# Talking-heads attention and a gated feed-forward on one core: the loads of the values and of the conversion go from SyncE's queue to GpSimd's, the mix weights from GpSimd to ScalarE

## The chip, the core and the metric

The kernel runs on one core of a Trainium2 chip. A core has five engines, each with its own queue that is worked through in order: TensorE (PE in the profile, with its weight loads as PEld), VectorE (DVE), ScalarE (ACT), GpSimd (POOL) and SyncE (SP, which issues DMAs and computes nothing). The metric is the device time of one execution in microseconds (us). Of the kernel before there are three runs, median 1788.36 us, 1786.55 to 1803.96, and one profiled execution.

## The reference

Attention over 8 batches of 12 heads, 448 tokens and 64 columns a head. A 12 by 12 matrix mixes the heads of the scores, a softmax follows, a second 12 by 12 matrix mixes the heads of the softmax, and then come the values. The result goes through a feed-forward layer of width 2048 whose gate is h minus tanh(h).

```python
scores = scale * np.matmul(q, k.transpose(0, 1, 3, 2))
scores = np.einsum('bhij,hg->bgij', scores, w_pre)
scores = scores - np.max(scores, axis=-1, keepdims=True)
attn = np.exp(scores)
attn = attn / (np.sum(attn, axis=-1, keepdims=True) + 1e-09)
attn = np.einsum('bhij,hg->bgij', attn, w_post)
attn_out = np.matmul(attn, v).astype(np.float32)
x = np.ascontiguousarray(attn_out.transpose(0, 2, 1, 3)).reshape(B * S, H * D)
h = x @ moe_w_in
g = h - np.tanh(h)
return (g @ moe_w_out).astype(np.float32)
```

## The kernel before

**Two stages.** The first, about 855 us, is the attention; the second is the feed-forward. Beside the attention the kernel also converts the weights of the feed-forward, which arrive as 64-bit numbers, into pairs of 32-bit parts and stores them to DRAM.

**Places.** The attention takes its tokens in 32 blocks (8 batches of 120, 120, 120 and 88 tokens) and these in 360 groups of at most 10 tokens, whose 12 heads fill 120 partitions. Two groups make a place; there are 180 places, and the loop over `p` writes the work of one after the other. A place `p` holds, in this order: the copy `at` of the mix of two places back out of PSUM (L570, or two L577 where a block ends, ScalarE); the issue of queued DMAs; the first head mix `premix(p)` (L521, TensorE, into `ps_p`); `norm(p - 1)`; `expo(p)`, which is two row maxima `mx` (L530, VectorE) and two exponentials `e` (L532, ScalarE, which also sum into `zs`); the jobs planned for this place (scores of a later block L477, transposes of q L443 or k L417, values L602, all TensorE); and the second head mix `mix(p - 1)` (L560, TensorE, into `ps_o`), whose result ScalarE copies at the start of the next place.

**The mix weights.** The softmax isn't divided in its full size. `norm` adds 1e-9 to the sums (L541), takes their reciprocal (L542, both VectorE) and multiplies it into the 60 columns of the second mixing matrix `wpost`, once for each half of the place's rows: the tile `wr` (L543, one GpSimd instruction for both halves). `mix` uses `wr` as a matmul operand, so its first matmul waits for `wr`; and as `ps_o` has one buffer, it waits for the copy `at` of the mix before.

**The conversion.** `narrow_steps` works on 56 chunks, two at a time with a third loading. Each chunk has eleven steps, spread over VectorE, ScalarE (L82, L85, L102) and GpSimd (L96, L98, L104), and about four such steps are placed at the end of each place. A chunk's load is the tile `cr` (three buffers), its two results go to DRAM as `ws`. L102 on ScalarE reads what GpSimd's L98 made.

**Queues.** DMAs are put on two Python lists, `queue` (loads of q, k and v, stores of x) and `slow` (the conversion's loads and stores), and `issue(6)` sends at most six of them at each place. The gathers `t<-s` (L510) that bring the scores of a group's tokens together are issued just before, straight on SP. All of it goes through SP's queue, at L369. What stands in front of the loop (`now()`, the first k, q and v tiles) goes through SP too.

At the end every engine's instructions are pinned to the order in which the code writes them (`in_order`), so the order on each engine is that of the program text.

Of the kernel before, what the change touches and what calls it, by code (L numbers as in the profile page):

```python
# [18 lines left out]
DRAM = bass.MemoryType.DRAM  # L19
# [129 lines left out]
def kernel_body(  # L149
# [11 lines left out]
    nc = tc.nc  # L161
    B, H, S, D = q.shape
    P = 128
# [9 lines left out]
    HP = GH * H  # L173
# [165 lines left out]
    with ExitStack() as st:  # L339
# [17 lines left out]
        kks, vts, krs, qrs, qbs, sts, ats = {}, {}, {}, {}, {}, {}, {}  # L357


        queue, slow, sent = [], [], {}  # L360

        def dma(dst, src, to=None):
            entry = [place[0], dst, src, None]
            (queue if to is None else to).append(entry)
            return lambda places=0: entry[3] is not None and entry[3] + places <= place[0]

        def send(x, engine):
            entry = x.pop(0)
            engine.dma_start(*entry[1:3])  # L369
            entry[3] = place[0]  # L370

        def issue(most):
            for x in (queue, slow):
                while x and most and x[0][0] < place[0]:
                    send(x, nc.sync)
                    most -= 1

        place = [0]
# [7 lines left out]

        def load_v(b, hq):
            t = kp.tile([CP, 4, NC, D], F32, name="vr", tag="vr", bufs=3)
            sent[b, hq, "v"] = dma(
                t.rearrange("p h c d -> p h (c d)"),  # L390
                v[b, 4 * hq : 4 * hq + 4].rearrange("h (p c) d -> p h (c d)", c=NC),
            )
            vts[b, hq] = t

        def load_q(i, t=None):
# [140 lines left out]
        def norm(p):  # L536
            zs = te[p][1]
            wr = gp.tile([P, 2, D], F32, name="wr", tag="wr", bufs=2)[:, :, :HP]
            for r in range(2):

                nc.vector.tensor_scalar_add(zs[:, 1, r : r + 1], zs[:, 0, r : r + 1], 1e-9)  # L541
            nc.vector.reciprocal(zs[:, 2], zs[:, 1])  # L542
            nc.gpsimd.tensor_mul(  # L543
                wr, wpost[:, :HP].unsqueeze(1).to_broadcast([P, 2, HP]), zs[:, 2].unsqueeze(2).to_broadcast([P, 2, HP])
            )
            te[p].append(wr)

        def mix(p):
# [101 lines left out]
        for hq in range(3):  # L650
            load_v(0, hq)
# [32 lines left out]
        for w in range(2):  # L684
            for at in AT[w]:
                x = repeat[:, w, at : at + HP].rearrange("p (i h) -> p i h", i=GH)
# [5 lines left out]
        wpre, wpost = [cst.tile([P, D], F32, name=x) for x in ("wpre", "wpost")]  # L692
        both = tmp_w[:, 2 * P : 2 * P + 4 * HP].rearrange("p (w a n) -> p w a n", w=2, a=2)
        for w in range(2):
            for a in range(2):
                if w == 0:
                    x = both[:, w, a].rearrange("p (i g) -> p i g", i=GH)
                    of, step = ps_w[:, w, :].unsqueeze(1).to_broadcast([P, GH, H]), [[H, GH], [0, H]]
                else:
                    x = both[:, w, a].rearrange("p (g i) -> p g i", i=GH)  # L700
# [68 lines left out]
        while halved:  # L769
            ready = sorted((x for x in halved if x[0] <= p), key=lambda x: (x[1], x[3:]))  # L770
            if ready:
                x = ready[0]
# [3 lines left out]
                if x[2] == kind and other and x[1] > p + 1:  # L776
                    x = other[0]
# [9 lines left out]
        for i, (b, m) in enumerate(blocks):  # L787
            p0 = first[i] // 2
            if i + 2 < len(blocks):
                p = at_s[i + 2, 0] - 1  # L790
                at_place(p, prep_q, i + 2, 0)
                at_place(p, prep_q, i + 2, 1)
                if i + 3 < len(blocks):
                    at_place(p + 1, load_q, i + 3)
            if b and m == 0:
                for hq in range(NP // 2):
                    at_place(p0 + 4 + hq, load_v, b, hq)
# [34 lines left out]
        for p in range(NPL + 3):  # L832
# [4 lines left out]
            for t in (2 * p + 4, 2 * p + 5):  # L837
                if t < NG:
                    gather(t)
            issue(6)  # L840
            if p == NPL + 1:
                for f in start.pop(p):
# [3 lines left out]
            if 1 <= p < NPL + 1:  # L846
                norm(p - 1)
# [100 lines left out]
```

## Time and profile before

| what | value |
|---|---|
| median of 3 runs | 1788.36 us (1786.55 to 1803.96) |
| the profiled execution's own time | 1788.92 us |
| its span, first to last instruction | 1787.2 us |
| granted TensorE clock, mean | 0.993 |
| busy: PE, PEld | 1751.0 us, 1425.6 us |
| busy: DVE, ACT, POOL | 1128.3 us, 1000.5 us, 320.1 us |
| HBM read and written | 245.37 MB, 47.19 MB |

The page gives each engine's busy time, groups of equal instructions by source line, and who waited for whom. `A L1 <- B L2: total, times, longest` in a list of waits means that engine A stood idle before its line L1 until B's line L2 had finished. In a timeline a row gives the start, the duration, the engine, the line, the operation, and at its end in brackets the idle time before it. A line named Lxxx is one of the kernel before.

### The profile page before, as it was taken

The page shows a single profiled execution, that of the slowest core. Times are in us where ns is not written, and L with a number is a line of the kernel's source. Part 1 is how long each engine was busy: PE and PEld are TensorE (multiplying, and loading weights), DVE is VectorE, ACT ScalarE, POOL GpSimd, SP SyncE. Part 2 cuts the span into 40 slices and gives each one's busy share as a digit, 9 for nine tenths or more (in the row PEclk, how much of TensorE's full clock was granted, in tenths as well). Part 3 has the DMA queues.
Part 4 walks back from the last instruction along what each step waited for, and adds up shares of the span by engine and source line. Part 5 has one row for each costly group of instructions (what it writes and reads, how often), then busy time and mean ns, then how long its engine had stood idle before and what let it go on. Part 6 is the DMA issues. An engine that isn't in the chain of part 4 may idle for free.

```text
span 1787.2 us, 41382 instructions
## 1 busy us (share of the span) xinstructions
PE 1751.0 (98%) x16572; PEld 1425.6 (80%) x16572; DVE 1128.3 (63%) x2362; ACT 1000.5 (56%) x2051; POOL 320.1 (18%) x417
## 2 busy tenths in 40 slices
PE   8999999999999999999999999999999999999998
PEld 6777777777777777777888888888888888888887
DVE  5676777777777767664556566565565565655555
ACT  5777877777777776765343443433434434444333
POOL 1333333333333333321010010000000000000000
PEclk9999999999999999999999999999999999999999
DMA  8668687777967687565655655655656655655651
GB/s 176 204 196 216 194 236 224 217 215 215 249 203 218 215 213 220 178 202 216 255 207 194 248 193 207 241 193 214 229 197 216 224 208 204 228 217 190 230 194 36
DMA packets 232816, 372.32 MB, mean 208 GB/s; under 512 B 98992, under 2 KB 207536, under 8 KB 218288
## 3 DMA queue, kind: packets, MB, share of 16 engines
q1 hardware_dynamic: 231740, 368.45, 64.0%
q8 instruction: 131, 2.15, 0.5%
q10 hardware_dynamic: 884, 1.22, 0.2%
q14 instruction: 61, 0.50, 0.1%
HBM read 245.37 MB, written 47.19 MB: 164 GB/s over the span
## 4 chain that ended last, share of the span: by engine, by line
PE 87%; DMA 4%; ACT 4%; DVE 3%; issue 1%; POOL 0%; SPq 0%; ACTq 0%; DVEq 0%; POOLq 0%
PE ps_o L560 13%; PE ps_h L257 8%; PE ps_h L258 8%; PE ps_h L262 8%; PE ps_m L602 8%; PE ps_p L521 7%; PE ya L305 6%; PE ya L302 6%; PE ya L303 6%; PE ps_q L477 5%; PE yb L305 3%; PE yb L303 3%; PE yb L302 3%; DMA t<-s 2%; PE ps_m L443 1%
## 5 line engine op out<-in xcount | busy, mean ns | idle before, releaser
L560 PEld LDWEIGHTS ps_o<-wr,e 60*112 60x112 f32 (+1 forms) x5760 | 306.2, 176 | 44.3 <-POOL wr L543 21.8
L560 PE MATMUL ps_o<-wr,e 60*112 60x60 f32 (+1 forms) x5760 | 315.5, 259 | 14.3 <-POOL wr L543 7.7
L530 DVE TENSOR_REDUCE mx<-ps_p 128x1 f32<-128x448 f32 x360 | 207.7, 619 | 163.9 <-PE ps_p L521 163.7
L532 ACT ACTIVATE e<-ps_p,mx 128x448 f32<-128x448 f32 x360 | 225.7, 634 | 101.9 <-DVE mx L530 99.4
L289 ACT CAST gh<-r 128x512 fp32r<-128x512 f32 x112 | 69.6, 621 | 372.6 <-DVE r L282 372.6
L258 PE MATMUL ps_h<-xl,w 128*128 128x512 f32 x672 | 264.4, 393 | 0.0
L257 PE MATMUL ps_h<-xh,w 128*128 128x512 f32 x672 | 264.3, 393 | 0.0
L570 ACT COPY at<-ps_o 112x960 f32<-112x960 f32 x156 | 153.7, 985 | 93.8 <-PE ps_o L560 93.2
L247 POOL TENSOR_TENSOR xl<-rx,xh 128x512 fp32r<-128x512 f32 x38 | 55.6, 1464 | 731.2 <-ACT xh L246 731.2
L521 PE MATMUL ps_p<-t,wpre 60*64 60x448 f32 (+1 forms) x1440 | 180.8, 569 | 3.9 <-DMA t<-s 2.7
L305 PE MATMUL ya<-w,gl 128*128 128x512 f32 x448 | 177.0, 395 | 0.7 <-DVE gl L290 0.7
L278 DVE SCALAR_TENSOR_TENSOR r<-qa,ps_h 128x512 f32<-128x512 f32 x112 | 77.1, 688 | 159.2 <-ACT t L275 159.2
L302 PE MATMUL ya<-w,gh 128*128 128x512 f32 x448 | 174.8, 390 | 1.0 <-ACT gh L289 1.0
L303 PE MATMUL ya<-w,gh 128*128 128x512 f32 x448 | 174.8, 390 | 0.0
L602 PEld LDWEIGHTS ps_m<-at,vr 112*64 112x64 f32 x3072 | 147.5, 137 | 31.0 <-ACT at L577 10.9
L262 PE MATMUL ps_h<-xh,w 128*128 128x512 f32 x672 | 170.6, 389 | 0.0
L602 PE MATMUL ps_m<-at,vr 112*64 112x120 f32 (+1 forms) x3072 | 161.6, 261 | 8.4 <-ACT at L577 3.1
L272 ACT ACTIVATE u<-ps_h 128x512 f32<-128x512 f32 x112 | 67.0, 599 | 152.9 <-PE ps_h L262 152.9
L262 PEld LDWEIGHTS ps_h<-xh,w 128*128 128x128 f32 x672 | 126.3, 188 | 26.3
L258 PEld LDWEIGHTS ps_h<-xl,w 128*128 128x128 f32 x672 | 127.5, 190 | 23.7
L257 PEld LDWEIGHTS ps_h<-xh,w 128*128 128x128 f32 x672 | 127.4, 190 | 23.4
L543 POOL TENSOR_TENSOR wr<-wpost,zs 128x120 f32<-128x120 f32 x180 | 70.2, 390 | 402.9 <-DVE zs L542 293.6
(93 smaller groups left out, 3038.0 us busy)
## 6 DMA issues: line engine op xcount, KB each, us to landing
w<-ws SPq DMA_DIRECT2D x112, 1536.0 KB
t<-s SPq DMA_DIRECT2D x342, 210.0 KB
cr<-in_moe_w_in_dram SPq DMA_DIRECT2D x24, 512.0 KB
cr<-in_moe_w_out_dram SPq DMA_DIRECT2D x32, 384.0 KB
vr<-in_v_dram SPq DMA_DIRECT2D x24, 448.0 KB
kr<-in_k_dram SPq DMA_DIRECT2D x23, 448.0 KB
out_dram<-ob SPq DMA_DIRECT2D x24, 384.0 KB
qr<-in_q_dram SPq DMA_DIRECT2D x23, 360.0 KB
```

Of the source, the lines that this page charges most:

```text
L257: nc.tensor.matmul(ph, wh[:, fs], xh, start=(c == 0), stop=False)
L258: nc.tensor.matmul(ph, wh[:, fs], xl, start=False, stop=False)
L262: nc.tensor.matmul(ph, wl[:, fs], xh, start=False, stop=(c == NK - 1))
L302: nc.tensor.matmul(y, gh[:, tok], wh[:, es], start=first, stop=False)
L303: nc.tensor.matmul(y, gh[:, tok], wl[:, es], start=False, stop=False)
L305: nc.tensor.matmul(y, gl[:, tok], wh[:, es], start=False, stop=last)
L521: nc.tensor.matmul(pss[r][halves[j], :], wpre[k, :], ts[j][k, :], start=True, stop=True)
L530: nc.vector.tensor_reduce(out=mx, in_=ps, axis=AX.X, op=ALU.max, negate=True)
L532: nc.scalar.activation(e, ps, AF.Exp, bias=mx, scale=1.0, accum_out=zs[:, 0, r : r + 1])
L560: nc.tensor.matmul(ps[:CP, j, c * GP : (c + 1) * GP].rearrange("p (h i) -> p h i", i=GI)[:, :, r * GH : (r + 1) * GH], e[k, c * CP : (c + ...
L570: nc.scalar.copy(ats[i0][:, :, :, at : at + 2 * GI].rearrange("p c h (j i) -> p j (c h) i", j=2), ps[:CP, :, : NC * GP].rearrange("p j (x ...
L602: nc.tensor.matmul(pv[j * D : (j + 1) * D, r, :n], vt[:, j, c, :], ats[i][:, c, 2 * hp + j, :n], start=(c == 0), stop=(c == NC - 1),)
```

## The change

Two things are moved. The loads of the values (`vr`, from the second batch on) and of the conversion's chunks (`cr`) are issued from GpSimd's queue instead of SP's; the stores of the conversion and every other DMA stay on SP. And `wr` is made by ScalarE, with two instructions of 60 columns that each take the reciprocal as a per-partition scale, instead of one GpSimd instruction.

```diff
-        queue, slow, sent = [], [], {}
+        queue, slow, sent, of_v = [], [], {}, []
...
         def issue(most):
             for x in (queue, slow):
                 while x and most and x[0][0] < place[0]:
-                    send(x, nc.sync)
+
+                    apart = x[0][1].space != DRAM and (x is slow or any(x[0] is y for y in of_v))
+                    send(x, nc.gpsimd if apart else nc.sync)
                     most -= 1
...
         def load_v(b, hq):
             t = kp.tile([CP, 4, NC, D], F32, name="vr", tag="vr", bufs=3)
+            before = len(queue)
             sent[b, hq, "v"] = dma(
...
+            of_v.extend(queue[before:])
             vts[b, hq] = t
...
             nc.vector.reciprocal(zs[:, 2], zs[:, 1])
-            nc.gpsimd.tensor_mul(
-                wr, wpost[:, :HP].unsqueeze(1).to_broadcast([P, 2, HP]), zs[:, 2].unsqueeze(2).to_broadcast([P, 2, HP])
-            )
+            for r in range(2):
+                nc.scalar.mul(wr[:, r, :], wpost[:, :HP], zs[:, 2, r : r + 1])
             te[p].append(wr)
```

ScalarE's queue around places 40 and 41 (213 to 219 us of the profile), before. Each row is a line, an operation, what it writes and reads, and its shape; `at` is the copy of a mix, `e` the exponentials, `cm`, `cr` and `cs` are steps of the conversion:

```order
L82 ACTIVATE cm<-cm 128x384
L570 COPY at<-ps_o 112x2x48x10
L532 ACTIVATE e,zs<-ps_p,mx 128x448 x2
L85 ACTIVATE cr<-cr 128x384
L102 CAST cs<-cm 128x384
L577 COPY at<-ps_o 112x48x10 x2
L532 ACTIVATE e,zs<-ps_p,mx 128x448 x2
```

The same stretch of ScalarE's queue in the changed kernel (its lines are numbered 3 or 4 higher):

```order
L82 ACTIVATE cm<-cm 128x384
L573 COPY at<-ps_o 112x2x48x10
L548 ACTIVATE wr<-wpost,zs 128x60 x2
L536 ACTIVATE e,zs<-ps_p,mx 128x448 x2
L85 ACTIVATE cr<-cr 128x384
L102 CAST cs<-cm 128x384
L580 COPY at<-ps_o 112x48x10 x2
L548 ACTIVATE wr<-wpost,zs 128x60 x2
L536 ACTIVATE e,zs<-ps_p,mx 128x448 x2
```

The two instructions of `wr` stand between the copy of the previous mix and the exponentials, at each of the 180 places.

GpSimd's queue where the values of a later batch are loaded (about 348 to 377 us of the profile), before:

```order
L104 TENSOR_TENSOR cl<-cm,cs 128x384
L543 TENSOR_TENSOR wr<-wpost,zs 128x2x60
L96 TENSOR_TENSOR cm<-cr,cs 128x384
L98 TENSOR_TENSOR cm<-cm,cr 128x384
L543 TENSOR_TENSOR wr<-wpost,zs 128x2x60
L104 TENSOR_TENSOR cl<-cm,cs 128x384
L543 TENSOR_TENSOR wr<-wpost,zs 128x2x60 x2
L96 TENSOR_TENSOR cm<-cr,cs 128x384
L543 TENSOR_TENSOR wr<-wpost,zs 128x2x60
L98 TENSOR_TENSOR cm<-cm,cr 128x384
```

The same stretch of GpSimd's queue in the changed kernel, where `vr` are values and `cr` a chunk of the conversion:

```order
L104 TENSOR_TENSOR cl<-cm,cs 128x384
L369 DMA vr<-in_v_dram 112x4x256
L96 TENSOR_TENSOR cm<-cr,cs 128x384
L98 TENSOR_TENSOR cm<-cm,cr 128x384
L369 DMA vr<-in_v_dram 112x4x256
L369 DMA cr<-in_moe_w_out_dram 128x768
L104 TENSOR_TENSOR cl<-cm,cs 128x384
L369 DMA vr<-in_v_dram 112x4x256
L369 DMA cr<-in_moe_w_out_dram 128x768
L96 TENSOR_TENSOR cm<-cr,cs 128x384
L98 TENSOR_TENSOR cm<-cm,cr 128x384
```

The weights are gone from GpSimd's queue, and loads now stand between its conversion steps: 77 in all, of which 56 are chunks and 21 are values.

## The prediction

> **What bounds the kernel now.** I read the page's busy times first, then busy time by stretch, split where the attention ends (columns: stretch, length, then busy time of PE, PEld, DVE, ACT and POOL with their instructions, the granted clock, DMA share, GB/s).
>
> ```profile
> span 1787.2 us, 41382 instructions
> PE 1751.0 (98%) x16572; PEld 1425.6 (80%) x16572; DVE 1128.3 (63%) x2362; ACT 1000.5 (56%) x2051; POOL 320.1 (18%) x417
> ...
> 30.00:830.00 800.00, 776.44 (x11394) 600.59 (x11388) 563.67 (x1524) 595.55 (x1357) 256.48 (x347) 0.99 0.72 210
> 870.00:1787.00 917.00, 911.00 (x4618) 773.12 (x4616) 533.69 (x773) 374.76 (x636) 52.92 (x36) 1.00 0.57 207
> ```
>
> TensorE is the bound in both stages. The change touches only the attention, and there TensorE is idle for 800.0 - 776.4 = 23.6 us. That is all that a removed wait can win; work added elsewhere costs something only where it makes TensorE wait. So the next view is the list of waits of PE and, below it, PEld.
>
> ```profile
> PE ps_o L560 <- POOL wr L543: 7.7, 10, 1.3
> PE ps_o L560 <- ACT at L570: 6.0, 9, 1.5
> ...
> PE ps_p L521 <- DMA t<-s: 2.7, 3, 1.6
> PE ps_m L602 <- DMA vr<-in_v_dram: 2.4, 2, 1.4
> ...
> PEld ps_o L560 <- POOL wr L543: 21.8, 23, 2.2
> ```
>
> The second head mix (L560) waits 7.7 us for GpSimd's weights and 6.0 us for ScalarE's copy of the mix before. The weight loader's 21.8 us is wider than TensorE's own loss, as earlier matmuls still run beneath it. The change removes the first wait and lengthens the path of the second.
>
> **The weights on ScalarE: their price.** No row of the trace is this operation, so its price comes from ScalarE's other rows, grouped by line with shapes kept apart; the last row is the GpSimd instruction that goes.
>
> ```profile
> L570 ACT COPY at<-ps_o 112x960 f32<-112x960 f32 x156 | 153.7, 985 | 93.8 <-PE ps_o L560 93.2
> L274 ACT ACTIVATE qb<-u,bias 128x512 f32<-128x512 f32 x112 | 79.3, 708 | 0.0
> L289 ACT CAST gh<-r 128x512 fp32r<-128x512 f32 x112 | 69.6, 621 | 372.6 <-DVE r L282 372.6
> L577 ACT COPY at<-ps_o 112x480 f32<-112x480 f32 x32 | 17.2, 583 | 9.3 <-PE ps_o L560 9.3
> L543 POOL TENSOR_TENSOR wr<-wpost,zs 128x120 f32<-128x120 f32 x180 | 70.2, 390 | 402.9 <-DVE zs L542 293.6
> ```
>
> From 480 to 960 columns a copy grows by (985 - 583) / 480 = 0.84 ns a column. From SBUF to SBUF, 512 columns take 621 ns, so 60 take 621 - 452 x 0.84 = 241 ns. A per-partition operand (`bias` in L274) adds 708 - 621 = 87 ns: 328 ns each. The pair is between 2 x 241 = 482 ns and 2 x 328 = 656 ns; I take 0.6 us, as the instruction does read such an operand and neighbours overlap a little. For 180 places that is 108 us more for ScalarE and 70 us less for GpSimd. The Trainium skill, "ScalarE: Activation LUTs", section "What ACT_TABLE_LOAD costs", has an activation at 186 ns plus 0.833 ns a column, 93 ns more for each per-partition operand, and an overlap of 93 ns between neighbours. The rows agree on the slope and the operand, and by that page the pair is 0.56 us and the total below 0.4 us lower.
>
> **The weights on ScalarE: who waits.** Four places show the kinds (start, duration, engine and line; the bracket is the idle time before).
>
> ```profile
> 213.41 0.96 ACT L570 COPY at<-ps_o 112x960 f32<-112x960 f32 x1
> 214.52 1.78 PE L560 MATMUL ps_o<-wr,e 60*112 60x60 f32 x32 [0.68 <-ACT at L570]
> ...
> 355.99 0.98 ACT L570 COPY at<-ps_o 112x960 f32<-112x960 f32 x1
> 357.74 0.39 POOL L543 TENSOR_TENSOR wr<-wpost,zs 128x120 f32<-128x120 f32 x1
> 358.18 0.51 PE L560 MATMUL ps_o<-wr,e 60*112 60x60 f32 x6 [0.41 <-POOL wr L543]
> ...
> 369.20 0.98 ACT L570 COPY at<-ps_o 112x960 f32<-112x960 f32 x1 [1.04 <-PE ps_o L560]
> 371.69 1.49 PE L560 MATMUL ps_o<-wr,e 60*112 60x60 f32 x28
> ...
> 514.14 0.98 ACT L570 COPY at<-ps_o 112x960 f32<-112x960 f32 x1
> 514.93 1.00 POOL L98 TENSOR_TENSOR cm<-cm,cr 128x384 f32<-128x384 f32 x1
> 515.89 0.39 POOL L543 TENSOR_TENSOR wr<-wpost,zs 128x120 f32<-128x120 f32 x1
> 516.34 1.39 PE L560 MATMUL ps_o<-wr,e 60*112 60x60 f32 x24 [1.33 <-POOL wr L543]
> ```
>
> At 514 the weights stood in GpSimd's queue behind a conversion step of 1.00 us, and TensorE was idle for 1.33 us. At 213 the copy is late: it ends at 214.37 and the mix starts 0.15 us later. In the changed kernel the mix can start at the copy's end plus 0.60 plus 0.15 us, as the pair stands right behind the copy.
>
> - At 514: 515.12 + 0.75 = 515.87 instead of 516.34, a gain of 0.47 of the 1.33 us. At 355: 356.97 + 0.75 = 357.72, before TensorE is free at 358.18 - 0.41 = 357.77, so all 0.41 us are won. Ten such waits at 0.44 us are 4.4 us; where the copy is as late as the weights there is less. I take 3 us won; the ends are 0 and 7.7.
> - At 213: the whole 0.60 us is added. With the nine waits of that row 5.4 us; the copy, which was late next, is late first. Its end could only be lower with the cheaper pair: 9 x 0.48 = 4.3.
> - At 369: 370.18 + 0.75 = 370.93, before 371.69. Here the scores between the two mixes cover the pair, and so do values, which take longer. In TensorE's order 11 mixes have only transposes before them; 355 is one and had 0.80 us between the copy's end and a free TensorE. These pay 0 to 0.6 us each, 0 to 6.6; I take 1 us.
>
> Sum for the weights: -3 + 5.4 + 1 = +3.4 us.
>
> The pair waits for the reciprocal, and behind it on ScalarE stand two exponentials, the score copies and the conversion; who waits for those is VectorE's sums and, a place later, TensorE.
>
> ```profile
> ACT e L532 <- DVE mx L530: 99.4, 143, 2.6
> ```
>
> In 143 places ScalarE stands still for 99.4 / 143 = 0.70 us for the row maxima, which hides the pair. In the other 37 the exponentials start up to 0.6 us later. Their sums are needed a whole place later, so I cost that at 0; if that cover were gone it would be 37 x 0.6 = 22 us.
>
> **The loads on GpSimd.** The rows are SP's DMA instructions (count: shortest/median/longest ns), one GpSimd step, ScalarE's wait for GpSimd, and three conversion steps in order of time.
>
> ```profile
> L369 SPq DMA_DIRECT2D cr<-in_moe_w_out_dram x32: 382/538/4801, 116.1 to 768.2; - x32
> L369 SPq DMA_DIRECT2D vr<-in_v_dram x24: 457/530/4240, 9.2 to 771.9; - x24
> ...
> L98 POOL TENSOR_TENSOR cm<-cm,cr 128x384 f32<-128x384 f32 x32 | 32.8, 1024 | 1.8
> ...
> ACT cs L102 <- POOL cm L98: 0.6, 1, 0.6
> ...
> 369.34 1.01 POOL L98 TENSOR_TENSOR cm<-cm,cr 128x384 f32<-128x384 f32 x1
> ...
> 373.74 0.53 ACT L102 CAST cs<-cm 128x384 fp32r<-128x384 f32 x1
> ...
> 517.03 0.51 ACT L102 CAST cs<-cm 128x384 fp32r<-128x384 f32 x1
> ```
>
> No row shows what a DMA costs GpSimd. The ends are SP's median, 0.5 us, and SP's longest for the values, 4.2 us; I take 1.2 us, near GpSimd's own step over the same tile (1.02 us), with a little more for the 112 x 4 pieces of a values load. The Trainium skill, "DMA: Bandwidth & Descriptors", section "Specifications", has about 1 us to the first byte on GpSimd's path and 0.6 us on SP's; by that the loads take an estimated 77 us of GpSimd, and the sum is the same. That makes 77 x 1.2 = 92 us, against 70 us that leave: GpSimd goes from 256 to some 278 of 800 us, no bound. What counts is order: a load ahead of L98 delays it, L102 on ScalarE waits for L98, and the exponentials stand behind L102. The cover is 373.74 - 370.35 = 3.4 us at 369 and 517.03 - 515.93 = 1.1 us at 514, on average 2.25; the waits measured are 0.6 us in all. A load of 1.2 us that takes the place of 0.39 us of weights adds 0.8 us, less than the thinner cover. A stretch with two loads in a row adds 2.4 and is not always covered: I charge 2 us. A values load also waits for the last use of its buffer by L602 a batch earlier; the code places it after that use, so I charge nothing.
>
> SP loses 77 issues of 0.53 us, 41 us. The gathers stand behind fewer loads, which can win at most the 2.7 + 2.4 us that TensorE waits for them and for values. I take 1 us; later landing could as well cost as much.
>
> **The sum.** +3.4 + 2 - 1 = +4.4 us on the profiled execution's own 1788.92 us (span 1787.2 us and 1.7 us around it), 1793.3 us. That execution is 0.6 us above the median of the runs, 1788.36, so I say 1793.
>
> **The rivals.**
>
> *Everything is hidden.* The pair falls into the 0.70 us of ScalarE's stillness, the 7.7 us and the 5.1 us for DMAs go: 1788.9 - 12.8 = 1776 us. For it: 143 of 180 places have that stillness. Against it: the pair stands behind the late copy, not behind the maxima. Chance 0.18.
>
> *GpSimd's loads are slow.* This is the case on the slower side. If a load takes 4.2 us there, then behind the 0.4 us that leaves and the mean cover of 2.25 us each of 77 makes L102 late by 1.55 us, 119 us in all. ScalarE has 800 - 595.6 - 108 = 96 us free in the stage, so 23 us pass to the exponentials and to TensorE: 1793 + 23 = 1816 us. It decides from about 3.9 us a load on. For it: the values' loads are cut into 448 pieces. Against it: SP needs 0.5 us for the same. The Trainium skill, "SBUF — State Buffer", section "Who interferes with whom", names a reason: a DMA issued from GpSimd has its descriptors written by GpSimd, which is locked out while VectorE runs in a mode that uses both ports; it gives 620 ns alone and 3100 ns beside such an operation, and advises SP or ACT instead. Nothing in the trace of before can show it. Chance 0.20.
>
> *ScalarE becomes the bound.* Its 595.6 + 108 = 704 of 800 us leaves little room; if the 37 late exponentials pass on their 22 us, 1793 + 22 = 1815 us. Against it: 96 us free. Chance 0.05.
>
> *The loads don't move.* The order shows them on GpSimd's queue, so I give this no chance.
>
> **How the numbers follow.** A difference of 1%, 18 us, is about what a measurement of this kernel tells from no change. The forecast has 0.57: 1793, by its own ends 1783 (all 7.7 won, 4.3 for the copies, no transposes late, loads free, 2 won on SP) to 1803 (nothing won, 5.4 for the copies, 6.6 for the transposes, 2 for the loads). Faster by over 1%, under 1770.5, asks for 18 of the 23.6 idle us and is beyond even the first rival: 0.04. Slower by over 1%, above 1806.2, is the second and third rival with most of their chance: 0.23. The rest, 0.73, is within 1%. The range 1779 to 1815 holds the forecast's ends, the upper part of the first rival and the lower half of the slower two; about 0.2 is left out, mostly above.
>
> **What would show it.** In the profile of the changed kernel the wait of L560 for POOL is gone and its wait for ACT is longer, some 10 to 12 us in total; the weights' row on ACT has 328 ns; ACT is busy for about 700 us of the stage; the DMA rows on POOL show 1 to 2 us; ACT's wait for L98 stays below 5 us. Loads above 3 us on POOL with a long wait of L102 would show the slow rival. A PE idle time in the attention below 15 us would show the first. The prediction is wrong if TensorE's idle time there (30 to 830 us) leaves 18 to 38 us, or if the busy time of its matmuls changes, for which I see no reason.

## The result and the profile after

The changed kernel takes 1808.64 us (median), the kernel before beside it 1788.61 us: a ratio of 1.0107, with a 95% interval of 1.0075 to 1.0138. Timed again later it was 1.0068 (1.0042 to 1.0093). Both intervals hold 0.75 to 0.93%. The two measurements put the cost of the change at some 20 and 12 us: a loss of about 1%, clear of zero, where the forecast had 4.4 us. Executions of one kernel spread over about 1%, and a profile is one of them: the one below, with 1820.08 us, is the longest of its kernel, so sizes are taken from the ratios and places from the profiles.

The page's totals of the changed kernel, and its busy times by stretch (columns as in the prediction):

```profile
span 1818.4 us, 41556 instructions
PE 1770.7 (97%) x16572; PEld 1438.9 (79%) x16572; DVE 1127.2 (62%) x2362; ACT 1083.0 (60%) x2411; POOL 298.8 (16%) x314
```

```profile
30.00:830.00 800.00, 770.40 (x10996) 593.83 (x10994) 549.33 (x1486) 657.31 (x1661) 234.76 (x242) 0.97 0.70 203
890.00:1818.00 928.00, 920.51 (x4659) 781.24 (x4657) 539.18 (x780) 377.33 (x640) 52.67 (x36) 1.00 0.58 208
```

The loss is nearly all in the attention: the last matmul of its mixes and values ends at 883.6 us instead of 855.4, which is 28.2 of the 31.2 us by which the span is longer. TensorE is idle from 30 to 830 us for 800.0 - 770.4 = 29.6 us instead of 23.6. But it also got through only 10996 matmuls in its 770.4 busy us, where it did 11394 in 776.4 before: 70.1 ns each instead of 68.1. The granted clock of the stretch fell with it: 0.97 instead of 0.99. The waits of the changed kernel:

```profile
PE ps_o L563 <- ACT wr L548: 14.2, 23, 1.4
PE ps_p L525 <- DMA t<-s: 12.2, 5, 4.1
PE ps_m L605 <- DMA vr<-in_v_dram: 3.1, 1, 3.1
```

The second head mix waits 14.2 us for the weights on ScalarE; before, it waited 7.7 for the weights and 6.0 for the copy, 13.7 together. What grew is the wait of the first head mix for its gathers, from 2.7 to 12.2 us. The two things that were moved take little time themselves. These are the weights on ScalarE and the loads on GpSimd (count: shortest/median/longest ns), and then ScalarE's wait for the conversion's step on GpSimd:

```profile
L548 ACT ACTIVATE wr<-wpost,zs x360: 328/344/425, 34.2 to 870.4; 128x60 f32<-128x60 f32 x180
```

```profile
L369 POOL DMA_DIRECT2D cr<-in_moe_w_out_dram x32: 557/580/804, 120.6 to 793.1; - x32
L369 POOL DMA_DIRECT2D cr<-in_moe_w_in_dram x24: 531/577/724, 12.4 to 687.6; - x24
L369 POOL DMA_DIRECT2D vr<-in_v_dram x21: 712/737/895, 152.1 to 801.0; - x21
```

```profile
ACT cs L102 <- POOL cm L98: 0.6, 2, 0.5
```

**One late gather, seen closely.** The changed kernel from 367 to 384 us in order of time (start, duration, engine and line), and then TensorE's busy time and granted clock in five neighbouring stretches of 3.4 us:

```profile
367.14 5.51 SPq L514 DMA_DIRECT2D t<-s  x4
...
367.70 0.75 POOL L369 DMA_DIRECT2D vr<-in_v_dram  x1
368.44 0.58 POOL L369 DMA_DIRECT2D cr<-in_moe_w_out_dram  x1
...
371.27 0.72 POOL L369 DMA_DIRECT2D vr<-in_v_dram  x1
371.97 0.58 POOL L369 DMA_DIRECT2D cr<-in_moe_w_out_dram  x1
...
373.44 11.35 SPq L369 DMA_DIRECT2D ws<-cs  x1
...
383.84 1.77 PE L525 MATMUL ps_p<-t,wpre 60*64 60x448 f32 x8 [4.09 <-DMA t<-s]
```

```profile
375.80:379.20 3.40, 3.30 (x64) 2.91 (x60) 0.36 (x1) 1.34 (x5) 0.79 (x1) 1.00 1.10 227
379.20:382.60 3.40, 0.55 (x12) 0.42 (x10) 1.51 (x6) 1.86 (x4) 0.00 (x0) 1.00 0.71 208
382.60:386.00 3.40, 2.16 (x10) 0.80 (x12) 0.33 (x1) 0.00 (x0) 0.00 (x0) 0.50 0.81 202
386.00:389.50 3.50, 3.50 (x32) 3.17 (x30) 2.63 (x8) 3.10 (x8) 0.00 (x0) 0.51 0.47 167
389.50:392.90 3.40, 3.40 (x54) 2.53 (x54) 1.57 (x3) 2.35 (x7) 1.00 (x1) 1.00 0.47 178
```

TensorE stands 4.09 us for a gather, and from 382.6 to 389.5 it works at half clock: in 3.5 busy us it does 32 matmuls there, afterwards 54 in 3.4. So a late gather is paid twice. When each DMA landed follows from the trace's semaphore events (issue, landing and time between, in us, worked out for this place and for the same place of the kernel before):

```
before, all on SP            after, SP and GpSimd
values  356.87  364.54  7.7  gather     SP    367.14  381.60  14.5
chunk   358.68  367.15  8.5  values     POOL  367.70  376.95   9.3
gather  360.73  368.38  7.7  chunk      POOL  368.44  379.33  10.9
gather  361.58  369.32  7.7  gather     SP    369.53  383.70  14.2
values  362.41  370.70  8.3  gather     SP    371.07  384.86  13.8
gather  363.03  371.49  8.5  values     POOL  371.27  381.95  10.7
```

On SP's line transfers landed in the order in which they were issued, so nothing issued behind a gather landed ahead of it. From GpSimd's line a values load and a chunk, issued after the gather, landed 4.7 and 2.3 us before it. The Trainium skill, "DMA: Bandwidth & Descriptors", section "Queues, rings and completion order", has each DMA engine take turns between the queues that have work, a packet at a time. The trace agrees in that transfers of both queues ran side by side; how long a turn is no run shows. Over the whole profile the median gather lands no later than before (4.3 us against 4.6); the longest takes 14.9 us instead of 9.9. Of the 360 gathers of the kernel before, none landed after a transfer that SP had issued behind it; in the changed kernel 28 landed after a load that GpSimd had issued behind them, and 17 took more than 9.9 us. Since a gather is issued two places ahead, only that tail reaches TensorE.

### The profile page after: what moved, and what is told of

Its sections match the earlier page's. It is cut to its first block, busy times and chain, and to the rows that moved or that the text cites. A ratio compares the mean times of both kernels' runs of the same rounds, so it can differ in the third digit from the quotient of the medians.

```text
span 1818.4 us, 41556 instructions
## 1 busy us (share of the span) xinstructions
PE 1770.7 (97%) x16572; PEld 1438.9 (79%) x16572; DVE 1127.2 (62%) x2362; ACT 1083.0 (60%) x2411; POOL 298.8 (16%) x314
## 3 DMA queue, kind: packets, MB, share of 16 engines
q0 software_dynamic: 8704, 34.80, 6.9%
q10 hardware_dynamic: 884, 1.22, 0.2%
## 4 chain that ended last, share of the span: by engine, by line
PE 83%; ACT 6%; DMA 5%; DVE 2%; issue 2%; SPq 0%; POOL 0%; ACTq 0%; DVEq 0%; POOLq 0%
PE ps_o L563 12%; PE ps_h L257 8%; PE ps_h L258 8%; PE ps_h L262 8%; PE ps_m L605 8%; PE ps_p L525 6%; PE ya L305 6%; PE ya L302 5%; PE ya L303 5%; PE ps_q L481 5%; PE yb L305 3%; PE yb L303 3%; PE yb L302 3%; DMA t<-s 3%; ACT e L536 2%
## 5 line engine op out<-in xcount | busy, mean ns | idle before, releaser
L563 PEld LDWEIGHTS ps_o<-wr,e 60*112 60x112 f32 (+1 forms) x5760 | 313.0, 179 | 45.3 <-ACT wr L548 30.5
L563 PE MATMUL ps_o<-wr,e 60*112 60x60 f32 (+1 forms) x5760 | 323.1, 263 | 14.3 <-ACT wr L548 14.2
L525 PE MATMUL ps_p<-t,wpre 60*64 60x448 f32 (+1 forms) x1440 | 184.3, 582 | 12.3 <-DMA t<-s 12.2
L605 PEld LDWEIGHTS ps_m<-at,vr 112*64 112x64 f32 x3072 | 149.7, 138 | 31.7 <-ACT at L580 11.4
L262 PEld LDWEIGHTS ps_h<-xh,w 128*128 128x128 f32 x672 | 126.1, 188 | 26.2
L258 PEld LDWEIGHTS ps_h<-xl,w 128*128 128x128 f32 x672 | 127.3, 189 | 23.6
L277 DVE TENSOR_SCALAR far<-u 128x512 f32<-128x512 f32 x112 | 47.9, 428 | 144.4 <-ACT u L272 137.0
```

The source lines that it names most:

```text
L258: nc.tensor.matmul(ph, wh[:, fs], xl, start=False, stop=False)
L262: nc.tensor.matmul(ph, wl[:, fs], xh, start=False, stop=(c == NK - 1))
L525: nc.tensor.matmul(pss[r][halves[j], :], wpre[k, :], ts[j][k, :], start=True, stop=True)
L563: nc.tensor.matmul(ps[:CP, j, c * GP : (c + 1) * GP].rearrange("p (h i) -> p h i", i=GI)[:, :, r * GH : (r + 1) * GH], e[k, c * CP : (c + ...
L605: nc.tensor.matmul(pv[j * D : (j + 1) * D, r, :n], vt[:, j, c, :], ats[i][:, c, 2 * hp + j, :n], start=(c == 0), stop=(c == NC - 1),)
```

## The experiments

The table has each kernel's time over that of the kernel before, and from its one profile TensorE's waits in us: for gathers, for values, for weights and copy of the second mix. The last two columns are TensorE's idle time between its first and last matmul, and the time lost at half clock (half of the length of the stretches whose granted clock is 0.5), both as differences to the profile of before (30.2 and 13.8 us).

| kernel | ratio (95% interval) | gathers | values | weights + copy | idle | half clock |
|---|---|---|---|---|---|---|
| before | 1 | 2.7 | 2.4 | 7.7 + 6.0 | 0 | 0 |
| changed | 1.0107 (1.0075 to 1.0138) | 12.2 | 3.1 | 14.2 | +11.1 | +22.4 |
| after2: changed, again | 1.0068 (1.0042 to 1.0093) | 10.1 | 4.2 | 14.1 | +10.2 | +12.2 |
| w_act: weights alone | 1.0014 (0.9991 to 1.0037) | 4.6 | 3.3 | 14.7 | +3.8 | +5.4 |
| l_pool: loads alone | 1.0061 (1.0040 to 1.0082) | 7.8 | 1.2 | 11.9 + 6.0 | +7.4 | +3.8 |
| l_conv: conversion's loads alone | 1.0066 (1.0045 to 1.0088) | 8.3 | 4.0 | 9.9 + 6.1 | +9.1 | +3.8 |
| l_conv_late | 1.0061 (1.0040 to 1.0082) | 7.3 | 8.1 | 8.4 + 5.4 | +8.4 | +13.3 |
| l_act: loads on ScalarE | 1.0070 (1.0046 to 1.0094) | 2.1 | 1.8 | 26.2 | +9.6 | +14.1 |
| a_stores | 1.0106 (1.0074 to 1.0139) | 15.2 | 0.6 | 14.5 | +12.3 | +12.4 |
| a_early | 1.0055 (1.0033 to 1.0076) | 4.7 | 4.9 | 16.6 | +9.0 | +18.8 |
| b_early | 1.0051 (1.0024 to 1.0079) | 1.6 | 12.1 | 8.7 + 2.6 | +7.6 | +15.9 |
| w_dve: weights on VectorE | 1.0031 (1.0012 to 1.0050) | 5.0 | 3.3 | 5.4 + 8.5 | +5.5 | +2.3 |
| gap_few | 1.0117 (1.0093 to 1.0142) | 2.0 | 3.7 | 20.3 + 6.0 | +11.6 | +8.6 |
| gap_fill | 1.0119 (1.0081 to 1.0156) | 5.5 | 1.1 | 11.4 + 6.3 | +2.4 | -1.7 |

The two last columns together account for the spans: for the changed kernel 11.1 + 22.4 = 33.5 us against a span that is 31.2 us longer, for the loads alone 7.4 + 3.8 = 11.2 against 13.2, for the changed kernel again 22.4 against 19.2. The two differ by 4.3 us at most, but for the last row, where TensorE has 13.9 us of work without use.

The gathers that took more than 9.9 us, the longest of the profile of before, tell the same apart: 0 to 2 in the six profiles in which SP issues every load, 5 to 28 in the six with chunks on GpSimd and gathers two places ahead, 8 in l_act and 15 in a_early.

**The two parts apart.** First the weights alone on ScalarE, all loads on SP:

```
-            nc.gpsimd.tensor_mul(wr, ...)
+            for r in range(2):
+                nc.scalar.mul(wr[:, r, :], wpost[:, :HP], zs[:, 2, r : r + 1])
```

> Only the weights are on ScalarE; all loads stay on SP. Theory 1 (the loads cost the time: with a queue of their own they run beside the gathers, TensorE waits for gathers and values, and each such gap is followed by a stretch of half clock): within 0.3% of before, 1785 to 1794 us, TensorE's waits for gathers and values stay near the 2.7 and 2.4 us of before, and the granted clock stays near 0.99 from 30 to 830 us. Theory 2 (the weights on ScalarE cost it: the second mixes start late, and gaps of 1 us and more there bring the half clock): 1800 to 1810 us, clock 0.97.

Then the loads alone on GpSimd, weights there as before:

```
+                    apart = x[0][1].space != DRAM and (x is slow or any(x[0] is y for y in of_v))
+                    send(x, nc.gpsimd if apart else nc.sync)
```

> Only the loads are on GpSimd; the weights stay on GpSimd too. Theory 1 (the loads): 1802 to 1812 us, TensorE waits about 10 us or more for gathers and values, clock about 0.97 from 30 to 830 us. Theory 2 (the weights on ScalarE): 1785 to 1794 us. A third view, that GpSimd now has loads, conversion steps and weights in one line, has the wait of the second mix for GpSimd's weights grow from 7.7 us by up to 77 x 0.6 us x 0.1, some 5 us, on top of either.

The weights come out at 1.0014, about 2.5 us and not to be told from nothing; the loads at 1.0061, 11 us. By the times theory 1 holds: the loads are what costs. Two of its signs missed for the loads alone: TensorE's waits for gathers and values came to 9.0 us where 10 or more were expected, and the clock from 30 to 830 us stayed at 0.99 where 0.97 was. In the rows, weights alone first, then loads alone:

```profile
PE ps_o L559 <- ACT wr L544: 14.7, 24, 1.4
PE ps_p L521 <- DMA t<-s: 4.6, 5, 1.6
```

```profile
PE ps_o L564 <- POOL wr L547: 11.9, 14, 1.9
PE ps_p L525 <- DMA t<-s: 7.8, 6, 2.5
PE ps_o L564 <- ACT at L574: 6.0, 9, 1.5
```

The third view was right as well: with loads ahead of them on GpSimd the weights are 4.2 us later (11.9 against 7.7), against 5.1 us more for the gathers, so the late gathers are not the whole loss of this kernel. The changed kernel doesn't pay that, as its weights are elsewhere; it pays in another place, below.

The changed kernel once more, held against the sum of the two parts:

> The changed kernel once more, beside the others and in more rounds, to hold it against the sum of its parts: loads alone 1.0061 and weights alone 1.0014 of before make 1.0075 if the parts add up. Above 1.0095 the two parts would make each other worse (the mixes that start behind ScalarE's copy and the late gathers falling into the same stretches of 3.4 us).

1.0068, and 1.0107 the first time: the sum of the parts, 1.0075, lies in both intervals, so no more than it is shown.

**Which loads.** Only the conversion's chunks on GpSimd (`apart` without `of_v`):

> Only the conversion's loads are on GpSimd; values and weights are as before. Theory 1: most of the loss of both loads, 1798 to 1810 us, as the conversion has 56 of the 77 loads and two of the three long waits for gathers in the changed kernel stand beside its loads. If the values' loads were the cause instead (they are cut small and TensorE waits for them directly), 1786 to 1794 us. Theory 2: 1785 to 1794 us.

1.0066: all of the loss is there without the values' loads, with 8.3 us of waits for gathers. So the cutting of the values into 448 pieces isn't needed for it.

**Too early, or side by side?** GpSimd waits for less than SP, and so issues a load sooner. Here its chunks stand behind the weights of their place:

```
+                    if apart:
+                        held.append(x.pop(0))
...
             norm(p - 1)
+            while held:
+                nc.gpsimd.dma_start(*held.pop(0)[1:3])
```

> As the run with only the conversion's loads on GpSimd (1.0066 of before), but each load stands behind the weights of its place in GpSimd's line, so that it is issued up to one place (4.4 us) later, nearer to where SP would issue it. Theory A (the loads run too early: GpSimd waits for nothing when SP still waits for its gathers, so they land on the gathers): back to 0.998 to 1.003 of before, with TensorE's waits for gathers below 4 us. Theory B (it is the sharing of the DMA engines by two queues, whenever the loads are issued): 1.005 to 1.008 of before, with waits for gathers of about 8 us.

1.0061, waits for gathers 7.3 us: theory B. A place earlier or later made no difference to the time; the chunks still ran in a queue beside the gathers' own. At the start of the kernel it does, though. Of the changed kernel and of the kernel before, stretches of 4 us (the last two columns are the DMA engines' busy share and GB/s):

```profile
18.00:22.00 4.00, 3.39 (x28) 2.10 (x25) 3.10 (x6) 2.61 (x6) 0.00 (x0) 1.00 1.07 335
22.00:26.00 4.00, 2.55 (x18) 1.47 (x17) 2.74 (x5) 2.19 (x5) 0.00 (x0) 1.00 1.03 239
```

```profile
18.00:22.00 4.00, 3.39 (x26) 2.10 (x25) 3.14 (x6) 2.64 (x6) 0.00 (x0) 1.00 0.79 134
22.00:26.00 4.00, 2.52 (x18) 1.44 (x17) 2.71 (x5) 2.16 (x5) 0.00 (x0) 1.00 0.31 119
```

With the weights gone from GpSimd's line nothing holds it, and the first three chunks are issued at 12.4 us instead of 44.0. They fill the DMA engines when the first gathers are issued (22.6 us), and TensorE stands 4.03 us for those, before 1.63. With the loads alone the first chunk goes at 42.1 us and that gap stays 1.64. Here the two parts make each other worse: the gap is 4.0 to 5.6 us in the four profiles in which GpSimd has loads and no weights, and 1.6 to 1.7 us in the ten others.

**Another queue, without GpSimd.** The changed kernel with its loads issued by ScalarE (`nc.scalar` for `nc.gpsimd`):

> As the changed kernel, but the 77 loads are issued by ScalarE instead of GpSimd, so they still leave SP's line, though not by GpSimd's path. If what costs time is that the loads run in another queue than the gathers, and so beside them: 1800 to 1815 us, with waits of TensorE for gathers of about 10 us. If it is GpSimd's path itself: 1787 to 1797 us with waits for gathers near 3 us. ScalarE's own issue of 77 loads at some 0.05 to 0.6 us each is 4 to 46 us, in its idle time for the most part.

By time the first reading, 1.0070; by the waits the second, as gathers cost 2.1 us. Neither holds as it was put: the loss has changed its place. ScalarE stands at its own loads for up to 5 us, and the weights stand behind them. In the place below it stood 5.39 us, by the trace until a store of the conversion (`ws<-cl`) had landed; only then did its load go, and the weights after it (TensorE's wait, and the place in order of time):

```profile
PE ps_o L563 <- ACT wr L548: 26.2, 27, 5.1
```

```profile
165.07 0.35 ACTq L369 DMA_DIRECT2D cr<-in_moe_w_out_dram  x1
165.53 0.58 ACT L548 ACTIVATE wr<-wpost,zs 128x60 f32<-128x60 f32 x2 [5.39 <-DMA ws<-cl]
165.92 3.06 PEld L563 LDWEIGHTS ps_o<-wr,e 60*112 60x112 f32 x32 [5.53 <-ACT wr L548]
```

Why gathers suffer less beside ScalarE's queue (9 of them were overtaken, where 28 were in the changed kernel) stays open. One difference shows in the queues' packets and megabytes, of this kernel and of the changed one:

```profile
q1 hardware_dynamic: 213932, 333.65, 55.9%
q10 hardware_dynamic: 18692, 36.02, 6.8%
```

```profile
q1 hardware_dynamic: 213932, 333.65, 55.8%
q0 software_dynamic: 8704, 34.80, 6.9%
```

From GpSimd the loads go in packets of 34.80 MB / 8704 = 4.0 KB; from ScalarE in 1.95 KB (34.80 MB in 18692 - 884 packets, as 884 packets and 1.22 MB are in q10 in any case). If queues take turns by packets, GpSimd's gets twice as much of each turn. That is argued and was not tried.

**What stands ahead of the gathers.** The store of 11.35 us in SP's line at 373 suggested that gathers are late behind the stores. With those on GpSimd too:

```
-                    apart = x[0][1].space != DRAM and (x is slow or any(x[0] is y for y in of_v))
+                    apart = x is slow or any(x[0] is y for y in of_v)
```

> The changed kernel with the 112 stores of the converted weights on GpSimd's queue too, so that SP's line holds only the gathers, queries, keys and the stores of x. If gathers come late because of what stands ahead of them in SP's line (the store that took 11.3 us at 373): TensorE's waits for gathers fall from 12.2 to below 4 us, 1.000 to 1.005 of before. If they come late because two queues share the DMA engines: the waits stay at 8 us or more, 1.008 to 1.015 of before.

1.0106, waits for gathers 15.2 us, more than ever. The long issue on SP is a sign of the crowding and not its cause: the gathers that TensorE waited for at 383 had been issued before that store. With more in the other queue the gathers waited longer (15.2 us against 12.2 and 10.1), though the time is no worse than the changed kernel's 1.0107 and 1.0068.

**Gathers a place earlier.** Three places ahead, with 8 buffers, and the scores planned a place sooner to match, first in the changed kernel, then in the one before:

```
-        RT = 6
+        RT = 8
...
-                hi = f1 // 2 - 3
+                hi = f1 // 2 - 4
...
-            for t in (2 * p + 4, 2 * p + 5):
+            for t in (2 * p + 6, 2 * p + 7):
```

> The changed kernel with every gather issued one place earlier (three places ahead of its use instead of two, 8 buffers instead of 6). If the late gathers cost what the changed kernel loses by its loads: the 12.2 us of waits for gathers go to below 3 us, and the time to 1.000 to 1.005 of before, the rest being the weights and the waits for values. If the gathers only show what is late anyway: no change, 1.008 to 1.012 of before.

> The kernel before with every gather issued one place earlier, with 8 buffers instead of 6. Its waits for gathers are 2.7 us in three places, each followed or not by 1.7 to 3.4 us at half clock: at best 2.7 + 5 us, 0.996 of before. If the earlier gathers push other transfers later (TensorE waits 2.4 us for values): 1.000 to 1.003.

In the changed kernel all late gathers are gone but the first, one of 4.7 us at 29; the time is 1.0055, against 1.0068 and 1.0107 without, no clear gain; it lies between what the two readings had, and neither holds as it was put. In the kernel before it is a loss, 1.0051, beyond what was expected: the gathers' waits fall to 1.6 us, and TensorE waits for values instead.

```profile
PE ps_m L602 <- DMA vr<-in_v_dram: 12.1, 5, 3.0
PE ps_o L560 <- POOL wr L543: 8.7, 10, 1.4
```

The schedule moves with the gathers (the scores must be ready a place sooner), and where transfers crowd, the one that was pushed back is the next to be late. Held against each other, the two runs say more than each alone: with every gather a place earlier, the kernel with the change and the one without differ by 0.0004 (1.0055 and 1.0051, each to within 0.003), where with the gathers at their old place they differ by 0.0068 to 0.0107. On top of the earlier gathers, which by themselves cost 0.5%, the change costs nothing that can be told from noise. That speaks for the lateness of the gathers as the way in which the loads cost time.

**The weights on VectorE.** One instruction beside the reciprocal (`nc.vector.tensor_mul`):

> The kernel before with the weights on VectorE in place of GpSimd (one instruction, next to the reciprocal that it needs; VectorE works 564 of the 800 us). On ScalarE the pair started only behind the late copy, and TensorE's waits for weights and copy together came to 14.7 us instead of 13.7. On VectorE the weights need no other engine: the wait for weights (7.7 us) goes, that for the copy (6.0 us) stays. Theory of the line (what counts is behind what the weights stand): 0.993 to 0.998 of before. Rival (the copy is late by then in any case, so where the weights are makes no difference): 0.998 to 1.003.

1.0031, just past the end of the rival's range. The weights are no longer late behind a copy or a conversion step, yet the two waits come to 5.4 + 8.5 = 13.9 us, as on GpSimd (13.7) and ScalarE (14.7).

```profile
PE ps_o L560 <- ACT at L570: 8.5, 13, 1.8
PE ps_o L560 <- DVE wr L543: 5.4, 6, 1.2
```

On all three engines the sum is 13.7 to 14.7 us: where the weights are made changed which row has the wait and hardly how much. What is late behind them on VectorE was not followed further.

**The price of a gap by itself.** In 12 places GpSimd makes the weights 8 times over:

```
+            for _ in range(8 if p % 15 == 7 else 1):
                 nc.gpsimd.tensor_mul(wr, ...)
```

> The kernel before, with GpSimd's weights instruction given 8 times instead of once in 12 of the 180 places (every 15th): 7 x 0.39 = 2.7 us more there, of which some 0.6 us is hidden, so that TensorE stands still 12 times for about 2.1 us. If only the idle time counts: 12 x 2.1 = 25 us over the kernel before of the same call (1.4%). If a gap of this size also makes the next stretch of 3.4 us run at half clock (1.7 us lost each, up to 3.4 when the stretch is 6.8 us): 12 x (2.1 + 1.7 to 3.4) = 46 to 66 us (2.6 to 3.7%), with a granted clock of about 0.95 from 30 to 830 us.

More was hidden than expected: the wait for weights rose by 20.3 - 7.7 = 12.6 us, about 1.05 us a place. The time rose by 1.17%, 21 us, so 12.6 us of waiting cost 21; the profile has 11.6 us more idle time and 8.6 more lost at half clock. The expected price per gap, 46 to 66 us in all, was too high: the gaps were about 1 us and not 2.1, and the clock fell in some of these places only. To see whether standing still is what lowers it, four matmuls without use ahead of these 12 mixes:

```
+            if p % 15 == 7:
+                for _ in range(4):
+                    nc.tensor.matmul(ps[:, 0, :P], ident, ident, start=True, stop=True)
```

> As the run with the weights given 8 times in 12 places (1.0117 of before), with 4 matmuls of the identity, some 1.25 us of TensorE's work that nobody needs, ahead of the mix in these 12 places. Its profile had 11.6 us more idle time than before and 8.6 us more lost at half clock. If the half clock comes from TensorE standing still, the filler keeps it working while it would wait anyway: the 11.6 us stay (as idle or as filler), most of the 8.6 us go, 1.006 to 1.009 of before. If the half clock has another cause: 1.011 to 1.014, as the filler saves nothing and in places outlasts the wait.

The time is 1.0119, so the filler wins nothing: the forecast for a clock lowered by idleness fails by its time. In the profile the idle time is 9.2 us and the half clock 10.3 us below the run without filler, and the filler's own 13.9 us take most of that back; but that profiled execution, 1804 us, was the shortest of its kernel, where the median is 1816.5, so it shows less than it seems to. As a proof of cause it is inconclusive; what speaks for that cause is the order in time, told below.

## Why the prediction came out as it did

The 1808.64 us lie inside the range of 1779 to 1815, but that is luck: the range reached so far up for loads that are slow on GpSimd and for ScalarE as the bound, and neither happened. The forecast itself, +4.4 us, was 8 to 16 us short of the 12 and 20 measured, and what was wrong is in two steps.

- *"SP loses 77 issues ... I take 1 us; later landing could as well cost as much."* This term was mis-sized: -1 us, with +2 us for GpSimd's side, where the loads alone cost 11. I asked what SP's line gains when loads leave it and not what the line had given: an order in which no load overtakes a gather issued before it. The six profiles with chunks on GpSimd and the gathers two places ahead have 7.3 to 15.2 us of waits for gathers; the five whose loads and gathers are all as they were (before, w_act, w_dve, gap_few, gap_fill) have 2.0 to 5.5.
- *"... or if the busy time of its matmuls changes, for which I see no reason."* That was the second step that failed, and it made the first one dearer: the matmuls took 70.1 ns each instead of 68.1, so by this sign of its own the prediction is wrong. A wait was costed at its own length. In the nine profiles with loads on another queue or gathers moved, idle time is 7.4 to 12.3 us above before and the half clock took another 3.8 to 22.4. TensorE's idle time in the attention, 29.6 us, lay well within the 18 to 38 us that the forecast allowed; that sign alone could not see the loss.
- *The price of the pair:* right. 344 ns each by the median and 105.6 us busy for 180 pairs, 0.59 us, where 0.6 was taken.
- *Who waits for the weights:* -3 + 5.4 + 1 = +3.4 us were forecast; the waits went from 13.7 to 14.2 us (14.7 with the weights alone), and the weights alone cost 1.0014, 2.5 us with an interval from -1.6 to +6.6. The mechanism is as told, the wait for ScalarE is 14.2 us where 10 to 12 were expected.
- *Exponentials at 0:* nothing speaks against it; with the weights alone ScalarE still stands 28.1 us for the row maxima, in 95 places, so there is cover left there.

```profile
ACT e L532 <- DVE mx L530: 28.1, 95, 2.8
```

- *The loads on GpSimd's side:* too dear. 0.58 and 0.74 us a load instead of 1.2, 49 us for the 77 where the prediction had 92 and, by the first-byte time that it cites, 77; and ScalarE's wait for the conversion's step stayed at 0.6 us, so the +2 us were 0. With that the rival of slow loads falls: it needed 3.9 us a load, and the longest of 77 took 0.895 us, with VectorE busy beside it for 549 of the 800 us. The lockout by VectorE that the Trainium skill's "SBUF — State Buffer", section "A bandwidth-pool intuition that's wrong (but worth ruling out)", describes at 3100 ns doesn't show here: no DMA that GpSimd issued took it more than 1.04 us in any run. Whether VectorE was ever in the mode that locks it out, the traces don't tell. That the 1816 us of this rival lie near the 1808.64 measured is chance.
- *Everything hidden* and *ScalarE as the bound* fall: the waits for the weights and the copy did not shrink, those for DMAs grew, and ScalarE was busy for 657 of the 800 us.

## What to carry to other kernels

A queue is also an order: on SP's queue at most one gather in a profile landed after a transfer issued behind it. With the other loads on GpSimd's queue 13 to 56 gathers did (9 with ScalarE's queue, where the loads held up ScalarE instead), so look at the longest landings and not at the median before loads are moved. On TensorE, count a wait of a microsecond or more at its length and about once more for the clock (0.4 to 2.1 times in the nine profiles); compare busy time per matmul between profiles, or half of the loss stays unseen. Where several steps are equally late, moving one of them to another engine (here the weights on three engines) can change the name in the row of waits and not the sum.

## What the hardware showed that was not expected

- **TensorE's clock fell after gaps of little over 1 us, on a fixed grid.** In the changed kernel's work it drops to 0.5 nine times, first at 27.6, 109.6, 321.2, 382.6 and 433.8 us, for 3.4, 6.8, 10.2 or 13.7 us; the starts lie on a grid of 3.41 us ((321.2 - 27.6) / 86 = 3.414). Between 40 and 915 us, over all 14 profiles, 26 stretches of that grid at full clock had TensorE busy for less than half of the time, and 25 of them were followed by half clock; between 50 and 70% busy it was 52 of 97; above 70% it was 3 of 3296. The Trainium skill, "TensorE: Matmul & The Clock Gate", section "Part 1: The HAM clock gate (the "warmup" mystery)", has such a free-running window of 3413 ns, and the runs agree on it. But by that page a whole idle window lowers the clock, and here a gap of 1.17 us did (before the mix at 433.5). Where a gap falls on the grid is a matter of chance, which fits the spread of about 1% among executions of one kernel.
- **A long issue on SP goes with late landings.** A store that takes 0.59 us to issue by the median took 11.35 us, with the DMA engines' share at 1.10 just then. It didn't wait for its data, which L102 had made by 370.2 us; its issue ended at 384.79 us, as the gather issued at 371.07 landed (384.86). Here the row marked crowding, and moving the stores away did not help.
- **No gain was found.** None of these kernels is faster than the one before: where an edit took one wait away, others grew: the earlier gathers in the kernel before, for one, won 1.1 us of waits for gathers and lost 9.7 on values.
